# State-space scan and mixture of experts: another order of the first block, gates behind the first masked scores, T3 behind the masked scores

## The chip, the cores and the metric

The kernel runs on one core of one Trainium2 chip. Its time is device microseconds of one execution; the number compared is the median over runs. All data are float32.

## The reference, cut to what matters

The reference is two blocks in a row. The first is a chunked state-space scan (4 sequences, 8 heads, 768 steps, head width 32, state width 16):

```python
for c in range(nc):                       # chunks along the sequence
    cum = np.cumsum(log(clip(a)), axis=-1)
    L = np.exp(cum_i - cum_j) * causal
    y_intra = ((C @ B.T) * L) @ x
    y_inter = (C @ state) * np.exp(cum)
    y[chunk] = y_intra + y_inter
    state = np.exp(sum) * state + (B * decay_from_j).T @ x
```

The second takes y as 3072 tokens of width 256 and runs four experts over all of them, weighted by normalised probabilities:

```python
p = domain_probs / (domain_probs.sum(-1, keepdims=True) + 1e-09)
for e in range(4):
    h = np.maximum(x @ w1[e], 0.0)        # 256 -> 1024
    out += p[:, e:e + 1] * (h @ w2[e])    # 1024 -> 256
```

## The kernel before

The scan works in chunks of 128 steps: 24 chunks, four of which make a block of 512 tokens, six blocks in all. All eight heads of a chunk are done together. The experts work on a block in eight steps (four experts, two halves of the hidden width each), so there are 48 steps, numbered n. The order on every engine is written out by hand; no scheduler changes it, and each engine's queue runs in that order.

A chunk c passes these functions. `load_tokens` and `load_decays` put its DMAs on SyncE's queue (SP). Chunks 0 and 1 read their decays straight from the input and clip them on VectorE (DVE); the later ones read decays that the kernel has clipped itself, once for all chunks: the tile `a_sb` is loaded, clipped, copied to `a_cut` (whose first column is zeroed), and `store_decays` writes both to DRAM (`acut_d`, `ac_d`) through ScalarE's (ACT's) queue. `masks` (ACT) makes two masked copies of C, `scores` (TensorE, PE) the products of C and B, in four PSUM tiles. `decays` makes the matrix L by a scan on DVE (L241, tile LT, 1024 columns) and, for all but the first chunk of a sequence, a second scan (dec). `masked` (L285, DVE) multiplies the scores by L, which frees the PSUM tiles of the scores. `outputs` (L297, L303, PE) gives y, which ACT copies to `yT`; `carry` (DVE) brings the state on.

The gates are the normalised probabilities: four DVE instructions (L200 to L203) normalise the tile `pr`, `store_gates` transposes it on PE, copies it on ACT and writes it to DRAM (`p_d`), and `load_gate(k, e)` reads the rows of block k and expert e back, spread over all partitions.

An expert step of the steady loop multiplies in Strassen's form: seven products into the PSUM banks X and Y (`fmul`, L358), copies of X on ACT (`snap`), sums on DVE (`total`, L370), the rectified and gated hidden values on DVE (`gated`, L380), and differences of those (`diff`, L387: T3, T1, T2, T4), which feed the seven products of the second matrix (`smul`, L442) in the next step. `sums(k)` makes four sums and differences of `yT` for block k on DVE (L336 to L339). The weights' sums (`sum_w1`, `sum_w2`) are made once, in the first block, on GpSimd (POOL), and written back to DRAM.

The first two steps of the first block are done plainly, without Strassen's form: `plain_first` (L406) into banks X and Y, `plain_gated` (two instructions of L380, which free X and Y), `plain_second` (L423). They are interleaved with the scan of chunks 0 to 3, since y of the first half of the block is there after chunk 1.

In the steady loop, four of a block's eight steps also take in a chunk of the next block: `masks` and `decays` early in the step, `scores` and `masked` near its end. The last two of the four score tiles stand in the banks X and Y, so that the next step's first product, which writes X, waits until `masked` has read it:

```python
scores(c_in, ((ps_att, "att"), (ps_att, "att"), (ps_f, "X"), (ps_f, "Y")))
masked(c_in, (2, 3, 0, 1))
```

Of the kernel before, what the change touches and what calls it, by code (L numbers as in the profile page):

```python
# [8 lines left out]
FP32 = mybir.dt.float32  # L9
# [8 lines left out]
def kernel(  # L18
# [75 lines left out]
    def load_tokens(c):  # L94
        xb = load.tile([P, W], FP32, tag="xb", name="xb")
        nc.sync.dma_start(out=xb, in_=xbc[c])
        st.setdefault(c, {})["xb"] = xb

    def load_decays(c, queue):
        ab = load.tile([P, NH * P], FP32, tag="ab", name="ab")  # L100
        cut, whole = (a, a) if c < DIRECT else (acut_d, ac_d)
        nc.sync.dma_start(out=ab, in_=cut[c].rearrange("h s -> (h s)").partition_broadcast(P))
        st.setdefault(c, {})["ab"] = ab
        if c % chunks_per_seq:
            ah = st[c]["ah"] = load.tile([HN, P], FP32, tag="ah", name="ah")
            queue.dma_start(out=ah, in_=whole[c].unsqueeze(1).to_broadcast([NH, N, P]))
# [55 lines left out]

    pr = const.tile([P, T // P, E], FP32, name="pr")
    a_sb = const.tile([NCH * NH // 2, 2, P], FP32, name="a_sb")
    nc.scalar.dma_start(out=pr, in_=probs)
    nc.scalar.dma_start(
        out=a_sb, in_=a.rearrange("c h s -> (c h) s").rearrange("(p r) s -> p r s", r=2))
    load_decays(0, nc.sync)
    load_tokens(0)
    load_tokens(1)  # L170
    load_decays(1, nc.sync)


    ident = const.tile([P, NH, P], FP32, name="ident")
# [20 lines left out]
    def clip(v):  # L195
        nc.vector.tensor_scalar(out=v, in0=v, scalar1=1e-6, scalar2=1.0, op0=ALU.max, op1=ALU.min)


    total = const.tile([P, T // P, 1], FP32, name="total")
    nc.vector.reduce_sum(total, pr, axis=mybir.AxisListType.X)  # L200
    nc.vector.tensor_scalar_add(total, total, 1e-9)
    nc.vector.reciprocal(total, total)
    nc.vector.tensor_mul(pr, pr, total.to_broadcast([P, T // P, E]))  # L203

    nc.gpsimd.tensor_scalar(  # L205
        out=a_sb, in0=a_sb, scalar1=1e-6, scalar2=1.0, op0=ALU.max, op1=ALU.min)
    a_cut = const.tile([NCH * NH // 2, 2, P], FP32, name="a_cut")
    nc.gpsimd.tensor_copy(a_cut, a_sb)
    nc.gpsimd.memset(a_cut[:, :, 0:1], 0.0)

    def store_decays():
        nc.scalar.dma_start(
            out=acut_d.rearrange("c h s -> (c h) s").rearrange("(p r) s -> p r s", r=2), in_=a_cut)
        nc.scalar.dma_start(
            out=ac_d.rearrange("c h s -> (c h) s").rearrange("(p r) s -> p r s", r=2), in_=a_sb)

    def store_gates():
        rows = T // P * E
        pp = ps_att.tile([rows, P], FP32, tag="att", name="pp")
        nc.tensor.transpose(pp, pr.rearrange("p i e -> p (i e)"), ident[:, 0])  # L220
        p_sb = const.tile([rows, P], FP32, name="p_sb")
        nc.scalar.copy(out=p_sb, in_=pp)
        nc.scalar.dma_start(out=p_d.rearrange("i e s -> (i e) s"), in_=p_sb)
# [3 lines left out]
    def load_gate(k, e):  # L227
        g = gate[k, e] = ffn.tile([P, CPB, P], FP32, tag="gate", name="gate", bufs=3)
        nc.sync.dma_start(out=g, in_=p_d[CPB * k:CPB * k + CPB, e].partition_broadcast(P))
# [31 lines left out]
    def masks(c):  # L261

        s = st[c]
        m = s["ctm"] = att.tile([HN, NT, P], FP32, tag="ctm", name="ctm")
        for t in range(NT):
            nc.scalar.mul(m[:, t], s["xb"][:, OCT:OCT + P], tmask[:, t:t + 1])  # L266
# [14 lines left out]
    def masked(c, qs):  # L281
        s = st[c]
        for q in qs:
            h = slice(NT * q, NT * q + NT)
            nc.vector.tensor_mul(s["MT"][:, h, 0:P], s["g"][q], s["LT"][:, h])  # L285
# [3 lines left out]
    def outputs(c, pool, tag):  # L289

        s = st[c]
        first = c % chunks_per_seq == 0
        w = P + N if c % chunks_per_seq < chunks_per_seq - 1 else P
        xb, MT = s["xb"], s["MT"]
        y = pool.tile([P, NT, P + N], FP32, tag=tag, name="y")
        if not first:
            nc.tensor.matmul(  # L297
                out=y[:, :, 0:P], lhsT=state["M"].rearrange("p q d -> p (q d)"),
                rhs=s["cts"], start=True, stop=False, skip_group_check=True)
        for t in range(NT):  # L300
            for q in range(NQ):
                h = NQ * t + q
                nc.tensor.matmul(  # L303
                    out=y[32 * q:32 * q + 32, t, 0:w], lhsT=xb[:, h * D:h * D + D],
                    rhs=MT[:, NT * q + t, 0:w], start=(first and t == 0), stop=True,
                    tile_position=(0, 32 * q), skip_group_check=True)
        k, i = divmod(c, CPB)
        if i == 0:
            yT[k] = ffn.tile([P, NT, BLK], FP32, tag="yT", name="yT")
        nc.scalar.copy(out=yT[k][:, :, i * P:i * P + P], in_=y[:, :, 0:P])  # L310
        if w > P:
            s["A"] = att.tile([P, NT, N], FP32, tag="A", name="A")
            nc.scalar.copy(out=s["A"], in_=y[:, :, P:])
# [70 lines left out]
    def diff(n, o, x, y):  # L384
        h = hid[n]
        h[o] = ffn.tile([P, JJ, HB], FP32, tag="h" + o, name="h" + o)
        nc.vector.tensor_sub(h[o], h[x], h[y])  # L387
# [23 lines left out]
    def plain_gated(n, b):  # L411
        gated(n, f"1{b}", "X")
        gated(n, f"2{b}", "Y")
# [106 lines left out]
    warm = const.tile([P, 1], FP32, name="warm")  # L520
    nc.scalar.mul(warm, tmask[:, 0:1], tmask[:, 0:1])
    homes = ((ps_s, "acc0"), (ps_s, "acc1"), (ps_att, "att"), (ps_att, "att"))
    masks(0)
    scores(0, homes)
    store_gates()
    store_decays()
    load_decays(2, nc.sync)
    load_gate(0, 0)
    load_w2(0)
    load_w1(1)  # L530
    load_chunk(3)
# [2 lines left out]
    masked(0, range(NQ))  # L534
    masks(1)
    outputs(0, ps_att, "att")
    load_gate(0, 1)
    load_w1(2)
    load_w2(2)
# [13 lines left out]
    decays(2)  # L553
    carry(1)
    masked(2, range(NQ))
    plain_gated(0, 1)
    masks(3)
    outputs(2, ps_att, "att")
    load_chunk(5)

    scores(3, homes)
    plain_first(1, 1)
    decays(3)
    carry(2)
    masked(3, range(NQ))
    plain_gated(1, 1)
# [4 lines left out]
    plain_second(0, 1, 2)  # L571
    plain_second(1, 1, 1)
    plain_second(1, 1, 2)
    plain_first(0, 2)
    plain_gated(0, 2)
    sums(0)
    carry(3)
    sum_w1(3)
    sum_w1(0)
    sum_w2(3)  # L580
# [6 lines left out]
    for n in range(PLAIN, NS):  # L587
        k, r = divmod(n, SPB)

        enter, exit = ({2: 0, 3: 1, 5: 2, 6: 3}, {3: 0, 4: 1, 6: 2, 7: 3}) if k == 0 else (  # L590
            {0: 0, 2: 1, 4: 2, 6: 3}, {1: 0, 3: 1, 5: 2, 7: 3})
        c_in, c_out = (CPB * (k + 1) + d[r] if r in d and k < NBLK - 1 else None
                       for d in (enter, exit))
        ending = r == 0 and k > 0
        e = r // JJ
        if r % JJ == 0 and n + JJ < NS:
            load_gate(*divmod(n // JJ + 1, E))
        if n + 2 < NS:
            load_w1(n + 2)
            load_w2(n + 2)  # L600
        opened(n)
        total(n, 1, "11")
        gated(n, "11", "z11")
        if c_in is not None:
            masks(c_in)
            decays(c_in)
        for m in {2: (), 3: (4, 5)}.get(n, (n + 2,)):
            sum_w1(m)
            sum_w2(m)
        if r == 1 and k > 0:  # L610
            leave(k - 1, 0, BLK, both)
        smul(n - 1, 1)
        fmul(n, 6)
        snap(n, 6)
        smul(n - 1, 3)
        if ending:
            keep(k - 1, 0)
        if c_out is not None:
            outputs(c_out, ps_att, "att")
        fmul(n, 5)  # L620
        fmul(n, 7)
        snap(n, 7)
        total(n, 7, "22")
        smul(n - 1, 7)
        smul(n - 1, 5)
        if n == PLAIN:
            sum_w2(0)
            sum_w2(1)
        if ending:
            keep(k - 1, 1)  # L630
        gated(n, "22", "z22")
        if c_out is not None:
            carry(c_out)
            if c_out + 2 < NCH:
                load_chunk(c_out + 2)
        fmul(n, 3)
        total(n, 6, "12")
        fmul(n, 4)
        gated(n, "21", "X")
        gated(n, "12", "z12")  # L640
        if r == SPB - 1 and k < NBLK - 1:
            sums(k + 1)
        smul(n - 1, 6)
        diff(n, "T3", "22", "12")
        smul(n - 1, 2)
        if c_in is not None:
            scores(c_in, ((ps_att, "att"), (ps_att, "att"), (ps_f, "X"), (ps_f, "Y")))
            masked(c_in, (2, 3, 0, 1))
        if ending:
            combine(k - 1, 0)  # L650
            combine(k - 1, 1)
        smul(n - 1, 4)
        diff(n, "T1", "12", "11")
        diff(n, "T2", "22", "T1")
        diff(n, "T4", "21", "T2")
        if ending:
            combine(k - 1, 2)
# [46 lines left out]
```

## Time and profile before

| what | value |
|---|---|
| median of 4 runs | 668.65 us |
| lowest and highest run | 665.47 and 669.65 us |
| the profiled execution's own time | 665.47 us |
| its span, first to last instruction | 663.7 us |
| TensorE matmuls busy | 640.4 us, 96% |
| VectorE busy | 491.6 us, 74% |
| ScalarE, GpSimd busy | 114.1 and 108.5 us |
| DMA | 128.62 MB, mean 194 GB/s |

The profiled execution is one of the four runs. The busy times are unions of the instructions' intervals as the hardware profiler recorded them; weight loads (PEld) overlap matmuls and are counted apart. In the profile a line such as "PE X L358" means TensorE writing tile X at line 358 of the kernel, and "<-DVE h L380" that the wait was ended by DVE's instruction at line 380.

### The profile page before, as it was taken

Reading aid. Unit: us, or ns where it says so; the run is one execution under the profiler, and the core shown is the slowest. Engines: PE = TensorE matmul, PEld = TensorE weight load, DVE = VectorE, ACT = ScalarE, POOL = GpSimd, SP = SyncE. Lnnn points to the kernel's source line nnn. Section 1 sums busy time; section 2 is a strip of 40 time slices with the busy share of each in tenths; the row PEclk is TensorE's granted clock in tenths of the full one; section 3 lists DMA queues with packets and bytes.
Section 4 is the critical chain, followed back from the end, with each engine's and each line's share of the span. In section 5 each row is a group of like instructions: output and inputs, shape, how many; then the busy total and the mean of one; then the engine's idle time right before and its main releaser. Section 6 shows DMA issues by size and latency. Waiting matters only on the chain.

```text
span 663.7 us, 8687 instructions
## 1 busy us (share of the span) xinstructions
PE 640.4 (96%) x3321; PEld 537.0 (81%) x3321; DVE 491.6 (74%) x785; ACT 114.1 (17%) x244; POOL 108.5 (16%) x156
## 2 busy tenths in 40 slices
PE   3989999999999999999999999999999999999995
PEld 1777787888888888888888888888888888888884
DVE  7746989698687688866878867779868767856554
ACT  2101111122112121221122111112211211111110
POOL 4485685011000002000003000002100000200000
PEclk9989999999999999999999999999999999999999
DMA  6986999636736544765372865554573542562102
GB/s 227 346 329 229 312 324 332 238 140 176 279 135 216 186 181 113 280 226 178 123 260 89 258 199 194 194 183 163 169 280 119 193 170 114 149 247 112 55 1 32
DMA packets 70937, 128.62 MB, mean 194 GB/s; under 512 B 29040, under 2 KB 52464, under 8 KB 70896
## 3 DMA queue, kind: packets, MB, share of 16 engines
q1 hardware_dynamic: 65824, 112.74, 49.6%
q0 software_dynamic: 2304, 14.68, 5.6%
q10 hardware_dynamic: 2768, 0.66, 0.5%
q8 instruction: 26, 0.43, 0.3%
q14 instruction: 15, 0.12, 0.1%
HBM read 109.99 MB, written 18.07 MB: 193 GB/s over the span
## 4 chain that ended last, share of the span: by engine, by line
PE 91%; DVE 6%; DMA 1%; POOL 1%; issue 0%; ACT 0%; ACTq 0%; DVEq 0%; POOLq 0%
PE acc L442 40%; PE X L358 24%; PE Y L358 18%; PE y L303 2%; PE acc L423 2%; PE g L275 2%; DVE h L380 2%; PE y L297 1%; DVE hT L387 1%; PE X L406 1%; PE Y L406 1%; DMA a_sb<-in_a_dram 1%; DVE LT L241 1%; POOL a_sb L205 0%; DVE z L370 0%
## 5 line engine op out<-in xcount | busy, mean ns | idle before, releaser
L370 DVE TENSOR_TENSOR z<-Y,snap 128x512 f32<-128x512 f32 x138 | 95.0, 688 | 125.9 <-ACT snap L365 99.8
L442 PE MATMUL acc<-hT,wt 128*128 128x256 f32 x736 | 183.4, 382 | 0.8 <-DVE hT L387 0.8
L365 ACT COPY snap<-X 128x512 f32<-128x512 f32 x138 | 80.8, 585 | 472.0 <-PE X L358 470.0
L442 PEld LDWEIGHTS acc<-hT,wt 128*128 128x128 f32 x736 | 138.2, 190 | 25.5 <-issue 6.3
L358 PE MATMUL X<-yS,wt 128*128 128x256 f32 x552 | 141.7, 379 | 0.0
L442 PE MATMUL acc<-h,wt 128*128 128x256 f32 x552 | 141.5, 379 | 0.0
L358 PEld LDWEIGHTS X<-yS,wt 128*128 128x128 f32 x552 | 104.9, 190 | 14.3
L442 PEld LDWEIGHTS acc<-h,wt 128*128 128x128 f32 x552 | 104.9, 190 | 14.3
L380 DVE SCALAR_TENSOR_TENSOR h<-z,gate 128x512 f32<-128x512 f32 x138 | 98.3, 712 | 3.1
L358 PE MATMUL Y<-yT,wt 128*128 128x256 f32 x368 | 95.2, 381 | 0.3 <-DVE z L370 0.3
L358 PEld LDWEIGHTS Y<-yT,wt 128*128 128x128 f32 x368 | 69.4, 191 | 11.5 <-DVE z L370 0.7
L387 DVE TENSOR_TENSOR hT<-h,hT 128x512 f32<-128x512 f32 x92 | 70.7, 768 | 3.2
L387 DVE TENSOR_TENSOR hT<-h,h 128x512 f32<-128x512 f32 x92 | 63.4, 711 | 1.4
L248 POOL TENSOR_TENSOR MT<-xb,LT 128x128 f32<-128x128 f32 x20 | 8.7, 437 | 317.6 <-issue 167.9
L241 DVE TENSOR_TENSOR_SCAN LT<-ab,ident 128x1024 f32<-128x1024 f32 x24 | 54.8, 2284 | 1.4 <-DMA ab<-acut_d 1.0
L358 PE MATMUL X<-yT,wt 128*128 128x256 f32 x184 | 48.6, 387 | 4.2 <-DVE h L380 2.6
L358 PE MATMUL Y<-yS,wt 128*128 128x256 f32 x184 | 49.4, 391 | 0.2 <-DVE z L370 0.2
L380 DVE SCALAR_TENSOR_TENSOR h<-X,gate 128x512 f32<-128x512 f32 x50 | 34.5, 690 | 15.3 <-PE X L406 8.6
L358 PEld LDWEIGHTS X<-yT,wt 128*128 128x128 f32 x184 | 35.1, 193 | 10.5 <-DVE h L380 3.0
L358 PEld LDWEIGHTS Y<-yS,wt 128*128 128x128 f32 x184 | 33.2, 189 | 8.8 <-issue 3.9
L285 DVE TENSOR_TENSOR MT<-g,LT 128x256 f32<-128x256 f32 x96 | 33.9, 415 | 6.8 <-PE g L275 6.7
L275 PE MATMUL g<-ctm,xb 32*128 32x256 f32 x192 | 20.8, 461 | 7.7 <-ACT ctm L266 7.6
(75 smaller groups left out, 311.4 us busy)
## 6 DMA issues: line engine op xcount, KB each, us to landing
wt<-w_d SPq DMA_DIRECT2D x80, 896.0 KB, 6.4
w_d<-wt POOLq DMA_DIRECT2D x16, 896.0 KB, 5.9
ab<-acut_d SPq DMA_DIRECT2D x22, 512.0 KB, 6.3
wt<-in_w_dram SPq DMA_DIRECT2D x32, 256.0 KB, 6.3
xb<-in_xbc_dram SPq DMA_DIRECT2D x24, 320.0 KB, 5.0
gate<-p_d SPq DMA_DIRECT2D x24, 256.0 KB, 6.4
out_dram<-ot SPq DMA_DIRECT2D x40, 64.0 KB, 2.0
ah<-ac_d SPq DMA_DIRECT2D x19, 64.0 KB
```

The source lines that it names most:

```text
L241: nc.vector.tensor_tensor_scan(out=LT, data0=s["ab"], data1=ident.rearrange("p h s -> p (h s)"), initial=0.0, op0=ALU.mult, op1=ALU.add)
L275: nc.tensor.matmul(out=g.rearrange("p t s -> p (t s)"), lhsT=s["xb"][k, OBT:OBT + P], rhs=s["ctm"][k].rearrange("p t s -> p (t s)"), start ...
L285: nc.vector.tensor_mul(s["MT"][:, h, 0:P], s["g"][q], s["LT"][:, h])
L303: nc.tensor.matmul(out=y[32 * q:32 * q + 32, t, 0:w], lhsT=xb[:, h * D:h * D + D], rhs=MT[:, NT * q + t, 0:w], start=(first and t == 0), s ...
L358: nc.tensor.matmul(out=f[bank][:, j], lhsT=wt1[n][:, w, j * P:j * P + P], rhs=rhs, start=(i in (1, 2, 5) and j == 0), stop=(j == JJ - 1), ...
L365: nc.scalar.copy(out=s, in_=first[n]["X"])
L370: nc.vector.tensor_add(z, first[n]["Y"], first[n][i])
L380: nc.vector.scalar_tensor_tensor(out=h, in0=first[n][src], scalar=0.0, in1=g.unsqueeze(1).to_broadcast([P, JJ, HB]), op0=ALU.max, op1=ALU. ...
L387: nc.vector.tensor_sub(h[o], h[x], h[y])
L406: nc.tensor.matmul(out=f[bank][:, j], lhsT=wt1[n][:, w, j * P:j * P + P], rhs=yT[k][:, i, cols], start=(i == 0 and j == 0), stop=(i == 1), ...
L423: nc.tensor.matmul(out=acc[k, u][:, half], lhsT=w2_op(n, w)[:, j], rhs=hid[n][f"{i + 1}{b}"][:, j], start=(begins and i == 0 and j == 0), ...
L442: nc.tensor.matmul(out=acc[k, u][:, half], lhsT=w2_op(n, w)[:, j], rhs=rhs[:, j], start=(begins and j == 0), stop=(n % SPB == SPB - 1 and ...
```

## The change

It moves five things in the first block, and one in the loop.

- The load of the decays `a_sb` becomes the only one ahead on ACT's queue; the probabilities' load moves to SP's queue, behind the tokens and decays of chunks 0 and 1. The decays of chunk 1 are loaded ahead of its tokens.
- The clip, copy and memset of `a_sb` and `a_cut` move from GpSimd to DVE, ahead of chunk 0's clip, and `store_decays` moves ahead of the first `masks` on ACT.
- The four instructions that normalise the probabilities move into `store_gates`, and that and the first gate load move behind chunk 0's `masked`, chunk 1's `masks` and chunk 0's `outputs`.
- `decays(3)` moves ahead of `plain_gated(0, 1)`, which itself moves from behind `masked(2)` to behind `scores(3)`.
- `sums(0)` and `carry(3)` move ahead of `plain_first(0, 2)` and `plain_gated(0, 2)`.
- In every step of the loop that takes in a chunk, the difference T3 moves behind `scores` and `masked`.

Lines behind the first edits move by two: L285 before is L283 after, L358 is L356, L380 is L378.

```diff
-    nc.scalar.dma_start(out=pr, in_=probs)
     nc.scalar.dma_start(
         out=a_sb, in_=a.rearrange("c h s -> (c h) s").rearrange("(p r) s -> p r s", r=2))
     load_decays(0, nc.sync)
     load_tokens(0)
+    load_decays(1, nc.sync)
     load_tokens(1)
-    load_decays(1, nc.sync)
+    nc.sync.dma_start(out=pr, in_=probs)
...
-    total = const.tile([P, T // P, 1], FP32, name="total")
-    nc.vector.reduce_sum(total, pr, axis=mybir.AxisListType.X)
-    nc.vector.tensor_scalar_add(total, total, 1e-9)
-    nc.vector.reciprocal(total, total)
-    nc.vector.tensor_mul(pr, pr, total.to_broadcast([P, T // P, E]))
-
-    nc.gpsimd.tensor_scalar(
-        out=a_sb, in0=a_sb, scalar1=1e-6, scalar2=1.0, op0=ALU.max, op1=ALU.min)
+    clip(a_sb)
+
     a_cut = const.tile([NCH * NH // 2, 2, P], FP32, name="a_cut")
-    nc.gpsimd.tensor_copy(a_cut, a_sb)
-    nc.gpsimd.memset(a_cut[:, :, 0:1], 0.0)
+    nc.vector.tensor_copy(a_cut, a_sb)
+    nc.vector.memset(a_cut[:, :, 0:1], 0.0)
...
     def store_gates():
+        total = const.tile([P, T // P, 1], FP32, name="total")
+        nc.vector.reduce_sum(total, pr, axis=mybir.AxisListType.X)
+        nc.vector.tensor_scalar_add(total, total, 1e-9)
+        nc.vector.reciprocal(total, total)
+        nc.vector.tensor_mul(pr, pr, total.to_broadcast([P, T // P, E]))
         rows = T // P * E
...
+    store_decays()
     masks(0)
     scores(0, homes)
-    store_gates()
-    store_decays()
     load_decays(2, nc.sync)
-    load_gate(0, 0)
     load_w2(0)
...
     outputs(0, ps_att, "att")
+    store_gates()
+    load_gate(0, 0)
     load_gate(0, 1)
...
     masked(2, range(NQ))
-    plain_gated(0, 1)
     masks(3)
     outputs(2, ps_att, "att")
     load_chunk(5)
 
     scores(3, homes)
+    decays(3)
+    plain_gated(0, 1)
     plain_first(1, 1)
-    decays(3)
     carry(2)
...
+    sums(0)
+    carry(3)
     plain_first(0, 2)
     plain_gated(0, 2)
-    sums(0)
-    carry(3)
...
         smul(n - 1, 6)
-        diff(n, "T3", "22", "12")
         smul(n - 1, 2)
         if c_in is not None:
             scores(c_in, ((ps_att, "att"), (ps_att, "att"), (ps_f, "X"), (ps_f, "Y")))
             masked(c_in, (2, 3, 0, 1))
+        diff(n, "T3", "22", "12")
```

## The prediction

> **What bounds the kernel now.** I read the page first, then a table of windows, then TensorE's waits, then the timeline of the first 110 us.
>
> ```profile
> PE 640.4 (96%) x3321; PEld 537.0 (81%) x3321; DVE 491.6 (74%) x785; ACT 114.1 (17%) x244; POOL 108.5 (16%) x156
> PEclk9989999999999999999999999999999999999999
> ```
>
> TensorE (PE) is busy 640.4 of 663.7 us, so a change of order can win at most the 23.3 us in which it is not, and time lost to its clock. The dip to 8 in the third slice (33 to 50 us) is the only one. The windows show where the idle time lies:
>
> ```profile
> 0.00:10.00 10.00, 1.65 (x9) 0.67 (x9) 6.45 (x24) 2.27 (x4) 6.28 (x17) 1.00 0.80 273
> 10.00:20.00 10.00, 7.46 (x55) 4.29 (x55) 8.63 (x15) 2.35 (x9) 2.97 (x5) 1.00 0.71 214
> 40.00:50.00 10.00, 7.43 (x28) 5.93 (x27) 6.43 (x10) 1.18 (x3) 8.87 (x14) 0.83 0.70 278
> 60.00:70.00 10.00, 8.89 (x55) 6.52 (x55) 9.24 (x14) 2.22 (x6) 2.49 (x4) 1.00 0.80 290
> 46.27:49.67 3.40, 3.15 (x7) 2.50 (x8) 0.80 (x2) 1.03 (x3) 2.97 (x5) 0.50 0.52 198
> 300.00:400.00 100.00, 100.00 (x530) 84.20 (x530) 77.20 (x126) 18.70 (x40) 6.92 (x9) 1.00 0.56 191
> ```
>
> First comes the length of the stretch, then PE, weight loads, VectorE (DVE), ACT and POOL; the last three are granted clock, DMA share and GB/s. From 110 us on PE is full (100.00 of 100), so T3's new place can win nothing there. Idle are 8.35 us of the first ten, 2.54 of the next, 2.57 between 40 and 50 and 1.11 between 60 and 70; nearly all the rest is the tail after 600, untouched. TensorE's waits say on whom:
>
> ```profile
> PE X L358 <- DVE h L380: 2.6, 1, 2.6
> PE X L358 <- DVE MT L285: 1.6, 3, 1.0
> PE y L297 <- DVE MT L285: 1.3, 1, 1.3
> ```
>
> The timeline has the three places (start, duration, instruction, idle time before it and who ended it):
>
> ```profile
> 4.02 0.25 DVE L200 TENSOR_REDUCE total<-pr 128x24 f32<-128x96 f32 x1 [2.12 <-DMA pr<-in_probs_dram]
> 5.03 0.68 DVE L196 TENSOR_SCALAR ab<-ab 128x1024 f32<-128x1024 f32 x1
> 9.69 0.68 DVE L196 TENSOR_SCALAR ab<-ab 128x1024 f32<-128x1024 f32 x1
> 15.30 1.19 PE L297 MATMUL y<-cts,M 128*128 128x256 f32 x2 [1.33 <-DVE MT L285]
> 16.52 2.29 DVE L241 TENSOR_TENSOR_SCAN LT<-ab,ident 128x1024 f32<-128x1024 f32 x1 [1.03 <-DMA ab<-acut_d]
> 38.81 0.69 DVE L380 SCALAR_TENSOR_TENSOR h<-X,gate 128x512 f32<-128x512 f32 x1 [8.62 <-PE X L406]
> 41.14 0.71 DVE L336 TENSOR_TENSOR yS<-yT 128x256 f32<-128x256 f32 x1
> 45.79 0.68 DVE L380 SCALAR_TENSOR_TENSOR h<-X,gate 128x512 f32<-128x512 f32 x1
> 46.52 2.07 PE L358 MATMUL X<-yT,wt 128*128 128x256 f32 x4 [2.57 <-DVE h L380]
> 62.64 0.69 DVE L387 TENSOR_TENSOR hT<-h,h 128x512 f32<-128x512 f32 x1
> 63.72 1.13 PE L358 MATMUL X<-yT,wt 128*128 128x256 f32 x4 [0.96 <-DVE MT L285]
> 78.47 1.13 PE L358 MATMUL X<-yT,wt 128*128 128x256 f32 x4 [0.29 <-DVE MT L285]
> 106.32 1.13 PE L358 MATMUL X<-yT,wt 128*128 128x256 f32 x4 [0.34 <-DVE MT L285]
> ```
>
> In the chain of waits PE runs without a gap from 15.30 to 40.51. So whatever delays 15.30 delays everything to 40, and what speeds DVE in between wins nothing.
>
> **The start: the gates go onto the chain.** Before, DVE normalised the gates at 4.02, waiting for chunk 0's decays anyway. Now they stand between chunk 0's masked scores (8.36 to 9.78) and chunk 1's clip, 9.69 before. From the first gate instruction to the next clip is 5.03 - 4.02 = 1.01 us. Behind them in DVE's queue stand the clip, chunk 1's scan, decay, carry and masked scores, on which PE waits at 15.30. Chunk 1's scan stood at 10.67, 0.98 after its clip; chunk 0's scan followed its clip by 0.93, so 0.05 was POOL's delay, which goes. PE's start moves by 1.01 - 0.05 = +0.96, to 16.26. Bounds: 0 if the gates find a hole; more if probs land late. The probs' DMA now stands on SP behind chunk 1's tokens, and by the order view its issue waits for a DMA landing (a_sb's, as I read its slot), at about 4 us. At the page's medians of 5.0 to 6.4 us a transfer lands at 9 to 10.4, and DVE asks for it at 9.78: 0 to 0.6 us more. I take 0, because the probs themselves took from 0.74 to 4.0 before.
>
> The clip and copy of a_sb move from POOL (3.12 + 0.39 us) to DVE. The DVE clips took 0.68 us for 1024 columns and 0.20 for 128, so about 0.27 for 256; twice that and a memset of 0.07 make 0.6. They lie in DVE's 2.12 us of idle time if a_sb lands as the probs did, by 4.0, since its DMA takes the probs' place at the head of ACT's queue; then chunk 0's clip stays at 5.03. If it lands at 5.91 as before, DVE ends them at 6.5 and the clip is 1.5 late. I take 0 and keep 1.5 for the range.
>
> The decays' stores now issue at about 4.7 instead of 10.71. SP sat behind them from 5.46 to 12.54; the load of chunk 2's decays, which landed at 16.40, should now issue at 6.5 to 8 and land by 14 (the page's 6.3). Chunk 2's scan then follows chunk 1's masked scores directly, at 15.49 + 0.96 = 16.45 against 16.52. DVE has paid for the gates with its 1.03 us of waiting; PE has not. The transposed gates (0.42 on PE, 0.26 on ACT) stand behind chunk 0's outputs, where PE waits until 16 anyway. POOL is free 1.5 us earlier, which wins nothing. On SP the first gate load stands behind more weight loads, at about 15; with 6.4 us it lands at 21 to 22.
>
> **Scan 3 ahead of the first gated tile.** DVE ends chunk 2's masked scores at 21.8, then scan (2.29) and decay (0.40) to 24.5, then h from X (0.68) to 25.2. Bank X is wanted by the next plain_first at 25.16 + 0.96 = 26.1. Cost 0, with 0.9 us of cover; the gate at 21 to 22 is in time too. The scan needs chunk 3's decays, behind chunk 3's tokens on SP: issued at 12 to 13, plus 6.3, about 19.
>
> **Sums and carry moved up.** The largest term. Before, DVE idled 8.62 us, then did h, h, the four sums and the carry (41.14 to 45.8), and only then the h from X that frees the bank for PE at 46.52. PE had ended its last plain_first at 43.95: 2.57 us idle. Now the 4.7 us of sums and carry run when chunk 3's yT is copied, at 32.0 + 0.96 = 33.0, until 37.7, still inside the idle time (plain_first(0,2) ends X at 38.8 + 0.96 = 39.8). The gated tiles follow PE one by one, and PE goes on at once: -2.57.
>
> The clock adds to it: the window of 46.27 to 49.67 was granted 0.50, hence the 0.83 of the window. In the chain the eight matmuls after 46.52 take 2.07 + 1.46 = 3.53 us, where the same eight take 0.86 + 0.86 = 1.72 later: 1.81 us, which goes with the gap. I take -1.81; the bound is 0, if a typical run does not fall into that state.
>
> [...] (That the start is cold shows in durations alone: the pair y L297 takes 1.19 us at 15.30 and 0.59 at 22.73.)
>
> **T3 down.** In four steps of the first block DVE does T3 between the gated tiles and the masked scores that free bank X. Moving T3 behind them takes it from PE's wait: 0.61 (its step to the next instruction, 62.64 to 63.25) of the 0.96, and the whole 0.29 and 0.34: -1.24. T3 itself ends 1.4 us later, which is covered: its matmuls stand at 71.13, T3 would end near 64.8. If that cover were gone PE would pay 1.4 a step. Bounds: 0 if DVE is the limit behind it (9.62 of 10 busy at 100 to 110), 1.6 at most.
>
> **Sum:** +0.96 - 2.57 - 1.81 - 1.24 = -4.66 us: the profiled execution's span 663.7 to 659.0 and its time, 1.8 above its span, 665.47 to 660.8. That execution is the fastest of four; their median is 668.65, and the same shift gives 664.0. Nothing in the profile explains the 3.2 us between them.
>
> **Rivals.** [...] (2) The start costs nothing, or T3 frees more: -5.6 or better, 663 or less. For: DVE's chain has hidden slack of 1.03. Against: PE's own wait at 15.30 names masked scores behind the gates. (3) Slower: SP's new waits hold chunk 3's decays. The scan now stands ahead of h, which frees X for PE; each microsecond of landing after 22.8 (21.8 + 0.9 cover) is one on PE, and beyond 22.8 + 4.66 = 27.4 the kernel is slower: at 31, 672.2. Against: they landed at 23.65 before although SP was blocked until 12.54. (4) That the change does not do what it says is excluded: the order view shows every move.
>
> **How the numbers follow.** Forecast (-3.4 to -5.6) 0.57; rival 1 0.27; rival 2 0.08; rival 3, with late probs, 0.08. A change under 0.5% (3.3 us) is about what a measurement of this kernel cannot tell from none. Faster by more: 0.57 + 0.08, less 0.02 for the edge, 0.63. Slower by more: 0.05. Within: 0.32. The range reaches from 661.0 (a gain of 7.6: rival 2 and the runs' spread) to 668.3 (rival 1 with a late a_sb); above and below it lies 0.2.
>
> **What would show it.** Right: PE's wait on h L380 of 2.6 us gone, no clock under 1 near 45, the PE start near 16.3, chunk 2's scan without DMA wait, waits of X on MT under 0.4 in all. Wrong: PE's first y L297 after 17.5 or before 15.4, a DVE wait on pr, a wait of LT on ab above 1 us near 22, or a gap of PE between 20 and 45.

## The result, and the profile after

The changed kernel's median is 666.73 us against 668.59 for the kernel before. The ratio of the two kernels' runs is 0.9976, with a 95% interval [0.9969, 0.9984]: 1.6 us faster. That is inside the 0.5% that was called no change. The direction was right; of the forecast 4.66 us about a third came. The profiled execution of after took 666.93 us (span 665.2), close to its median. The profiled execution of before was the fastest of its four, so absolute positions in the two traces can't be subtracted as if both were usual.

The page's lines and the windows of after, with the columns as before:

```profile
PE 641.0 (96%) x3321; PEld 537.4 (81%) x3321; DVE 494.4 (74%) x788; ACT 114.1 (17%) x244; POOL 111.0 (17%) x153
PEclk9999999999999999999999999999999999999999
```

```profile
40.00:50.00 10.00, 10.00 (x47) 8.57 (x46) 3.92 (x7) 1.17 (x3) 6.71 (x11) 1.00 0.46 184
60.00:70.00 10.00, 9.34 (x57) 7.10 (x57) 9.66 (x15) 2.42 (x7) 4.12 (x6) 1.00 0.74 262
46.27:49.67 3.40, 3.40 (x16) 2.75 (x15) 1.27 (x2) 1.17 (x3) 2.92 (x6) 1.00 0.51 205
300.00:400.00 100.00, 99.83 (x529) 84.01 (x528) 76.05 (x126) 18.16 (x39) 6.91 (x9) 1.00 0.55 186
```

The hole between 40 and 50 us is gone (7.43 busy before, 10.00 now), the dip of the clock with it (0.50 granted from 46.27 to 49.67 before, 1.00 now). What is new is small and far away: between 300 and 400 us PE was busy 100.00 and now is 99.83. The waits of after say on whom; the first line is DVE's, the others PE's (total in us, count, longest in us):

```profile
DVE MT L283 <- PE g L273: 20.2, 18, 1.1
PE Y L356 <- DVE z L368: 3.3, 8, 0.6
PE X L356 <- DVE MT L283: 0.7, 2, 0.5
```

and the same of before:

```profile
DVE MT L285 <- PE g L275: 6.7, 17, 0.4
PE Y L358 <- DVE z L370: 0.5, 2, 0.3
```

The wait on h of 2.6 us is gone, as forecast, and X waits for MT 0.7 us instead of 1.6; under 0.4 was forecast. But PE's wait for z, from which bank Y comes free, went from 0.5 to 3.3 us, and DVE's own wait for the scores from 6.7 to 20.2. The timeline of after around the start (start, duration, instruction, idle time and what ended it):

```profile
5.04 0.29 DVE L196 TENSOR_SCALAR a_sb<-a_sb 96x256 f32<-96x256 f32 x1 [3.15 <-DMA a_sb<-in_a_dram]
5.70 0.69 DVE L196 TENSOR_SCALAR ab<-ab 128x1024 f32<-128x1024 f32 x1
10.36 0.24 DVE L212 TENSOR_REDUCE total<-pr 128x24 f32<-128x96 f32 x1
11.37 0.69 DVE L196 TENSOR_SCALAR ab<-ab 128x1024 f32<-128x1024 f32 x1
16.92 1.19 PE L295 MATMUL y<-cts,M 128*128 128x256 f32 x2 [3.30 <-DVE MT L283]
17.20 2.29 DVE L239 TENSOR_TENSOR_SCAN LT<-ab,ident 128x1024 f32<-128x1024 f32 x1
```

The gates take 11.37 - 10.36 = 1.01 us of DVE's chain, just as computed, and the probabilities were there in time. Chunk 2's scan has no DMA wait any more. But a_sb landed at 5.04 and not by 4.0, so chunk 0's clip begins 0.67 later than 5.03, and y starts at 16.92, 1.62 after the 15.30 of before.

### The profile page after: what moved, and what is told of

Its sections match the earlier page's. It is cut to its first block, busy times and chain, and to the rows that moved or that the text cites. A ratio compares the mean times of both kernels' runs of the same rounds, so it can differ in the third digit from the quotient of the medians.

```text
span 665.2 us, 8685 instructions
## 1 busy us (share of the span) xinstructions
PE 641.0 (96%) x3321; PEld 537.4 (81%) x3321; DVE 494.4 (74%) x788; ACT 114.1 (17%) x244; POOL 111.0 (17%) x153
## 4 chain that ended last, share of the span: by engine, by line
PE 87%; DVE 8%; issue 1%; ACT 0%; DVEq 0%
PE acc L440 38%; PE X L356 22%; PE Y L356 17%; DVE hT L385 3%; PE g L273 2%; PE acc L421 2%; PE y L301 2%; DVE MT L283 1%; PE X L404 1%; PE y L295 1%; DVE z L368 1%; PE Y L404 1%; DVE h L378 1%; DVE LT L239 1%; DVE o L468 0%
## 5 line engine op out<-in xcount | busy, mean ns | idle before, releaser
L356 PE MATMUL X<-yS,wt 128*128 128x256 f32 x552 | 141.7, 379 | 0.0
L356 PEld LDWEIGHTS X<-yS,wt 128*128 128x128 f32 x552 | 104.9, 190 | 14.3
L378 DVE SCALAR_TENSOR_TENSOR h<-z,gate 128x512 f32<-128x512 f32 x138 | 98.7, 715 | 3.1
L356 PE MATMUL Y<-yT,wt 128*128 128x256 f32 x368 | 94.8, 380 | 0.4 <-DVE z L368 0.3
L356 PEld LDWEIGHTS Y<-yT,wt 128*128 128x128 f32 x368 | 68.6, 190 | 11.9 <-DVE z L368 1.2
L356 PE MATMUL Y<-yS,wt 128*128 128x256 f32 x184 | 49.4, 391 | 3.0 <-DVE z L368 3.0
L283 DVE TENSOR_TENSOR MT<-g,LT 128x256 f32<-128x256 f32 x96 | 34.0, 416 | 20.4 <-PE g L273 20.2
L356 PE MATMUL X<-yT,wt 128*128 128x256 f32 x184 | 47.4, 380 | 0.7 <-DVE MT L283 0.7
L356 PEld LDWEIGHTS Y<-yS,wt 128*128 128x128 f32 x184 | 33.2, 189 | 11.9 <-DVE z L368 5.2
L378 DVE SCALAR_TENSOR_TENSOR h<-X,gate 128x512 f32<-128x512 f32 x50 | 34.5, 691 | 9.5 <-PE X L356 5.7
L356 PEld LDWEIGHTS X<-yT,wt 128*128 128x128 f32 x184 | 34.8, 190 | 6.1 <-DVE MT L283 1.5
```

Of the source, the lines that this page charges most:

```text
L356: nc.tensor.matmul(out=f[bank][:, j], lhsT=wt1[n][:, w, j * P:j * P + P], rhs=rhs, start=(i in (1, 2, 5) and j == 0), stop=(j == JJ - 1), ...
L378: nc.vector.scalar_tensor_tensor(out=h, in0=first[n][src], scalar=0.0, in1=g.unsqueeze(1).to_broadcast([P, JJ, HB]), op0=ALU.max, op1=ALU. ...
```

## The experiments

Results of all twelve, each against runs of the kernel before on the same chip (its median was 668.58 to 668.75 there). After itself stands at 0.9976 [0.9969, 0.9984].

| kernel | median us | ratio to before |
|---|---|---|
| e1: after, T3 back in its old place | 665.69 | 0.9944 [0.9923, 0.9966] |
| e2: before, T3 down alone | 669.86 | 1.0011 [0.9995, 1.0027] |
| e3: before, sums and carry up alone | 666.67 | 0.9964 [0.9949, 0.9979] |
| e4: before, the start's edits alone | 668.55 | 0.9997 [0.9977, 1.0016] |
| e5: after, T3 down in block 0 alone | 664.39 | 0.9947 [0.9931, 0.9964] |
| e6: e5 with 68 idle matmuls at the start | 667.62 | 0.9983 [0.9974, 0.9993] |
| e7: e1 without normalising | 664.31 | 0.9941 [0.9928, 0.9954] |
| e8: before without normalising | 668.13 | 1.0003 [0.9986, 1.0021] |
| e9: e1 with 31 idle matmuls | 664.03 | 0.9933 [0.9912, 0.9955] |
| e10: e1, scan 3 back too | 666.13 | 0.9964 [0.9946, 0.9982] |
| e11: e5 with 31 idle matmuls | 662.18 | 0.9909 [0.9888, 0.9931] |
| e12: e11, T3 down in block 0's first loop step alone | 662.92 | 0.9914 [0.9894, 0.9934] |

**e1 and e2: T3 undone, and T3 alone.** The edit of e1 on after; e2 makes the opposite one on before.

```diff
         smul(n - 1, 6)
+        diff(n, "T3", "22", "12")
         smul(n - 1, 2)
...
             masked(c_in, (2, 3, 0, 1))
-        diff(n, "T3", "22", "12")
```

> The changed kernel with T3 back in its old place. Theory A (T3's new place costs time: DVE now idles until the scores are there, and total's z, which frees bank Y, comes late in the steady loop): TensorE's waits on z fall from 3.3 us to under 0.8, DVE's idle time before MT from 20 to about 7 us, waits of X on MT rise from 0.7 to about 1.5; about 2.4 us faster than the changed kernel, 664.3, ratio to the kernel before 0.9935. Rival A' (the waits on z come from TensorE being earlier after the sums were moved): z waits stay near 3 us, X on MT rises by 0.8, 667.5, ratio 0.9985.

> The kernel before with T3 alone moved behind the masked scores. Theory A: waits on z of about 3 us appear in the steady loop, those of X on MT fall from 1.6 to 0.7: about 2 us slower than before, 670.6, ratio 1.003. Rival A': 0.9 us to 1.2 us faster, 667.5, ratio 0.998, z waits as before (0.5).

Taking T3 back makes after faster: 0.9944 against 0.9976, intervals just apart, 2.1 us. T3 alone makes before slower by 0.7 us, an interval that reaches to no change. So T3's move, forecast to win 1.24 us, loses 2.1 us in the changed kernel; on top of before the loss is smaller and not clear of noise. The waits of e1 and then of e2 show the exchange:

```profile
DVE MT L283 <- PE g L273: 6.7, 17, 0.4
PE X L356 <- DVE MT L283: 2.1, 3, 1.5
PE Y L356 <- DVE z L368: 0.5, 2, 0.3
```

```profile
DVE MT L285 <- PE g L275: 21.1, 20, 1.1
PE Y L358 <- DVE z L370: 3.6, 8, 0.8
PE X L358 <- DVE MT L285: 0.5, 1, 0.5
```

Wherever T3 stands behind the masked scores, X's wait shrinks by 1.1 to 1.4 us and Y's wait on z is about 3 us longer. How it comes about is seen in DVE's timeline near 144 us, in the first step of the second block, before:

```profile
144.55 0.69 DVE L387 TENSOR_TENSOR hT<-h,h 128x512 f32<-128x512 f32 x1
145.63 1.42 DVE L285 TENSOR_TENSOR MT<-g,LT 128x256 f32<-128x256 f32 x4 [0.40 <-PE g L275]
...
151.21 0.68 DVE L370 TENSOR_TENSOR z<-Y,snap 128x512 f32<-128x512 f32 x1
```

and after:

```profile
145.42 1.42 DVE L283 TENSOR_TENSOR MT<-g,LT 128x256 f32<-128x256 f32 x4 [1.12 <-PE g L273]
146.76 0.68 DVE L385 TENSOR_TENSOR hT<-h,h 128x512 f32<-128x512 f32 x1
147.36 0.42 DVE L460 TENSOR_TENSOR u<-acc,kept 128x256 f32<-128x256 f32 x1
...
151.60 0.68 DVE L368 TENSOR_TENSOR z<-Y,snap 128x512 f32<-128x512 f32 x1
```

The masked scores wait for the scores on PE, not for DVE. T3 (0.69 us) filled that wait; now the wait stands empty (0.40 becomes 1.12) and T3 comes behind it. All that follows on DVE, the next step's z among it, is that much later relative to PE, z frees Y, and PE waits:

```profile
152.34 1.13 PE L356 MATMUL Y<-yS,wt 128*128 128x256 f32 x4 [0.55 <-DVE z L368]
257.61 1.13 PE L356 MATMUL Y<-yS,wt 128*128 128x256 f32 x4 [0.60 <-DVE z L368]
362.94 1.13 PE L356 MATMUL Y<-yS,wt 128*128 128x256 f32 x4 [0.17 <-DVE z L368]
467.79 1.13 PE L356 MATMUL Y<-yS,wt 128*128 128x256 f32 x4 [0.18 <-DVE z L368]
```

Before, the first of these four groups had no wait, at 151.95. These four lines are all that T3's move costs PE in the later blocks, 1.5 us in sum; the other four of the eight waits on z, 1.8 us in sum, lie in the first block. Of the 16 steps of the later blocks that take in a chunk, PE waits in four, one in each block: its first step, in which DVE also adds up the output of the block before (u in the timeline above) and has no idle moment between T3 and z. In the other twelve T3 comes late too, but PE does not wait; there DVE has idle time further on, and between 110 and 600 us its wait for ACT's copies (snap) fell from 79.9 to 70.4 us.

**e3, e4 and e10: sums, start, scan.** e3 moves only `sums(0)` and `carry(3)`; e4 makes only the first three points of the change on before; e10 takes scan 3 back out of e1.

```diff
+    sums(0)
+    carry(3)
     plain_first(0, 2)
     plain_gated(0, 2)
-    sums(0)
-    carry(3)
```

```diff
-    nc.scalar.dma_start(out=pr, in_=probs)
...
+    nc.sync.dma_start(out=pr, in_=probs)
...
+    clip(a_sb)
...
+    store_decays()
     masks(0)
     scores(0, homes)
-    store_gates()
-    store_decays()
...
     outputs(0, ps_att, "att")
+    store_gates()
```

```diff
     masked(2, range(NQ))
+    plain_gated(0, 1)
...
     scores(3, homes)
-    decays(3)
-    plain_gated(0, 1)
     plain_first(1, 1)
+    decays(3)
```

> The kernel before with only sums(0) and carry(3) moved up. Theory: the gap of 2.57 us before the first Strassen step is gone, and with it the half-speed stretch near 46 us: 2.6 us faster if only the gap counts in a typical run, 4.4 if the clock does too: 664.2 to 666.0, ratio 0.9934 to 0.9961; TensorE's first y L297 stays at 15.3. Rival (the stall only moves: DVE is late for the gated tiles or the loop waits later): less than 1.5 us faster, above 667.1.

> The kernel before with only the start changed (loads, decays' clip and stores, gates). Theory B (the gates cost 0.96 us and the late landing of a_sb 0.67 us, on TensorE's path): first y L297 at 16.9, about 1.6 us slower, 670.2, ratio 1.0024. Rival (DVE's wait for chunk 2's decays, 1.03 us, was on the path, so the start costs 0 to 0.6): 668.6 to 669.2, ratio under 1.001.

> The changed kernel with T3 back and with scan 3 and the first gated tile in their old order, so the start and the sums alone are left of the change. My prediction's cover: scan 3's new place costs and wins nothing, ratio 0.9944 as with it. Rival (scan 3's place wins, because masked scores of chunk 3 come earlier; start and sums alone measured 0.9997 and 0.9964): 0.996.

The sums win 2.4 us [1.4, 3.4], not 4.38. The start's edits cost nothing: -0.2 us, with an interval from -1.5 to +1.1 that just holds the forecast +0.96 too. Together (e10) they give what the sums give alone. Putting scan 3 up as well (e1 against e10) wins 1.3 us by the ratios, whose intervals overlap, so that they don't show it, and 0.7 by the two traces: e1's X at 79.27 us is 0.82 ahead of e10's at 80.09, of which 0.15 is an earlier first y (17.12 against 17.27).

Two traces say more. This is the timeline of e3, which has the start of before:

```profile
5.70 0.25 DVE L200 TENSOR_REDUCE total<-pr 128x24 f32<-128x96 f32 x1 [3.80 <-DMA pr<-in_probs_dram]
6.71 0.69 DVE L196 TENSOR_SCALAR ab<-ab 128x1024 f32<-128x1024 f32 x1
16.93 1.19 PE L297 MATMUL y<-cts,M 128*128 128x256 f32 x2 [1.26 <-DVE MT L285]
```

The probabilities landed at 5.70 here, against 4.02 in the profile of before, DVE reached the first clip 1.7 us later, and y began at 16.93, where after has it too (16.92). In e2, the other trace with all of before's start, the probabilities landed at 5.86 and y began at 17.09; in the five traces with after's start and no idle matmuls (after, e1, e4, e5, e10) it began between 16.92 and 17.66. The start that the forecast took for usual was an early one.

PE's waits of e4 and then of e3 show why the sums won less:

```profile
PE X L356 <- DVE h L378: 1.7, 1, 1.7
PE X L356 <- DVE MT L283: 1.7, 2, 1.4
```

```profile
PE X L358 <- DVE MT L285: 2.7, 3, 1.8
```

The stall on h was 1.7 in e4 (1.8 in e2), not 2.57. It is as long as DVE makes it: the four sums and the carry took 4.65 us in the trace of before (41.14 to 45.79), 3.79 in e4 and 3.87 in e2, because some of the same instructions took longer there, for a reason that no run shows. And once it is gone (e3), X waits for MT 2.7 us, where before had 1.6 and e4 1.7: PE arrives earlier at chunk 4's masked scores, about 64 us, and DVE is not ready. The clock's part was smaller too. The eight matmuls of the first Strassen step, up to the start of the next ones, took 49.89 - 46.52 = 3.37 us in before and 48.82 - 46.90 = 1.92 in after: 1.45 us for the half-speed stretch, not 1.81.

```profile
49.89 1.89 PE L423 MATMUL acc<-h,wt 128*128 128x256 f32 x8
```

```profile
46.90 1.03 PE L356 MATMUL X<-yT,wt 128*128 128x256 f32 x4
48.82 1.89 PE L421 MATMUL acc<-h,wt 128*128 128x256 f32 x8
```

A stall of 1.75 and up to 1.45 for the clock, less the 1.1 that comes back at chunk 4's masked scores, make up to 2.1. The measured 2.4 [1.4, 3.4] allows that; no run separates the three.

**e5: T3 down in the first block alone.**

```diff
+        if k > 0:
+            diff(n, "T3", "22", "12")
         smul(n - 1, 2)
...
+        if k == 0:
+            diff(n, "T3", "22", "12")
```

> The changed kernel with T3 behind the masked scores in the first block alone, in its old place from the second block on. Theory A (in the steady loop T3 fills the time in which DVE waits for the scores; in the first block DVE is behind TensorE and bank X is the wait): waits on z under 1.5 us, of X on MT under 1 us; faster than the version with T3 back everywhere (ratio 0.9944) by 0.5 to 1.2 us, ratio 0.993. Rival (T3's gain in the first block is lost to the wait on z that follows there): no faster than 0.9944.

0.9947 against e1's 0.9944. PE's waits of e5:

```profile
PE Y L356 <- DVE z L368: 1.8, 4, 0.5
PE X L356 <- DVE MT L283: 0.7, 2, 0.5
```

X's 2.1 become 0.7 and Y's 0.5 become 1.8: in the first block alone the new place gives what it takes. What after loses, 1.9 us by the ratios (0.9947 to 0.9976), is lost in the later blocks, where X had no wait that T3's move could cut; the four waits there make 1.5 of it.

**e7 and e8: no normalising.** Both leave out the four instructions that normalise the probabilities (`reduce_sum`, add, `reciprocal`, `tensor_mul`), e7 in e1, e8 in before.

```diff
-    nc.vector.reduce_sum(total, pr, axis=mybir.AxisListType.X)
-    nc.vector.tensor_scalar_add(total, total, 1e-9)
-    nc.vector.reciprocal(total, total)
-    nc.vector.tensor_mul(pr, pr, total.to_broadcast([P, T // P, E]))
```

> The changed kernel with T3 back, without the four instructions that normalise the probabilities (that part of the computation is left out). Theory B1 (in the new place they are on the path by 0.95 us): first y L295 0.95 us earlier, 16.0, about 0.9 us faster than with them (ratio 0.9944), 0.993. Rival (DVE waits anyway): 0.9944.

> The kernel before without the four normalising instructions (that part of the computation is left out). Theory B2 (in a usual run the probabilities land at about 5.7 us, after chunk 0's decays, so the instructions hold chunk 0's clip by about 1.2 us in their old place too; the profiled run, where they ran at 4.02, is an early one): first y L297 near 15.8 instead of 17, 1 us faster than before, ratio 0.9985. Rival (they lie in idle time, as I predicted): ratio 1.000, y L297 unchanged.

Without them y starts at 15.93 in e7 (17.12 in e1) and at 16.17 in e8 (16.93 in e3, which shares before's start). So these instructions stand on the path of the first y in both places, for about 1.0 us (1.2, of which 0.2 is an earlier first clip in e7) and 0.8 us: the move replaced one cost by another of nearly the same size. Whether an earlier first y is worth time stays open: e8 gained nothing (1.0003), with a stall on h of 2.3 us, while e7's trace is still 1.2 us ahead of e1's at 63 us, with a ratio (0.9941) too wide to tell it.

**e6 and e9: idle matmuls at the start.** The traces of after and e1 had shown the first expert matmuls slow: eight of them took 3.33 and 3.78 us, where eight take 1.99 later. Matmuls on zeros, written into the still unused bank X, fill PE's idle time before and between the first scores: 28, 12 and 28 of them in e6 (on e5), 12, 6 and 13 in e9 (on e1).

```diff
+    heat(12)        # nc.tensor.matmul on zeros, 128 columns each
     scores(0, homes)
+    heat(6)
...
     scores(1, homes)
+    heat(13)
```

> The same with 68 idle matmuls (128x128 by 128 columns of constants, into bank X, result unused) on TensorE ahead of its first scores, behind them, and behind chunk 1's scores, where TensorE waits anyhow. Theory C (TensorE's clock, granted in full only at 23.7 to 26.3 us, makes the stretch from 17 us on last longer, half of 6.5 to 9 us): full clock before 17 us, y, scores and plain_first at full speed from 17 on, 3 to 4.5 us faster than without, ratio 0.987, if DVE keeps up. Rival C' (DVE's scans and masked scores are the bound there, so a faster TensorE waits for them): less than 1.5 us faster, new waits of y on MT.

> The changed kernel with T3 back in its old place, and idle matmuls cut to fit TensorE's waits: 12 ahead of the first scores, 6 behind them, 13 behind chunk 1's scores (each takes two records of 0.11 us at the full clock, 0.21 at half). Theory C (the half-speed start costs time): full clock from about 6 us, first y L295 at 16.9 to 17.2 as without them, first Strassen step at 44 instead of 46.9 to 48.3, 2 to 4 us faster than without (ratio 0.9944): 0.989 to 0.991. Rival C' (DVE binds in that stretch): gaps of over 1 us on TensorE between 20 and 44, ratio above 0.993.

e6 was too large: each call is two records, the idle matmuls pushed the first scores from 7.6 to 9.9 us and y to 21.8, and the kernel lost against e5. In e9 the first scores, at 7.52 us, took 0.71 us, where after's, at 7.40, took 1.24, and the first Strassen step came at 44.50 instead of e1's 48.25, 3.75 us earlier; the time gained only 0.0011, within the error. The timeline and the window of e9 show where the lead went:

```profile
61.76 1.13 PE L356 MATMUL X<-yT,wt 128*128 128x256 f32 x4 [2.46 <-DVE MT L283]
```

```profile
62.80:66.20 3.40, 3.40 (x10) 2.69 (x9) 3.30 (x6) 1.18 (x3) 0.57 (x1) 0.50 0.71 249
```

PE came to chunk 4's scores early and waited 2.46 us for DVE instead of 1.48 (e1), and behind that wait the clock was halved for 3.4 us.

**e11 and e12: both together.** If that wait eats the lead, T3 down at that step, where DVE is late, should free it: e11 is e5 with e9's idle matmuls, e12 the same with the move in one step alone:

```diff
-        if k > 0:
+        if n > PLAIN:
             diff(n, "T3", "22", "12")
...
-        if k == 0:
+        if n == PLAIN:
             diff(n, "T3", "22", "12")
```

> The 31 idle matmuls as fitted, with T3 behind the masked scores in the whole first block, in its old place after it. The first fitted version won 3.9 us by 45 us and lost 2.5 of it at the first Strassen step's end, where bank X waits 2.46 us for the masked scores. If DVE's queue is what is late there, T3's new place takes 0.65 us off that wait and costs up to 1.5 in waits on z later in the block: ratio 0.993 to 0.996 (0.9933 without). If the half-speed window after that wait goes too: 0.991.

> The same with T3 behind the masked scores in the first Strassen step alone, the one where bank X waits longest. If the loss on z comes from the later steps only, this keeps the 0.65 us and costs nothing: ratio 0.992; first wait of X on MT near 1.8 instead of 2.46, waits on z under 0.6. Rival (what T3 leaves is taken by z of the next step at once): 0.9933 or above.

PE's waits of e11:

```profile
PE X L356 <- DVE MT L283: 0.8, 1, 0.8
PE Y L356 <- DVE z L368: 1.1, 3, 0.6
```

e11 took 662.18 us, 0.9909 [0.9888, 0.9931], e12 the same within the error: about 6 us faster than before and 4.5 faster than after. X's wait of 2.46 us is 0.77 in e11, and the half-speed stretch behind that wait is gone there: the clock column shows 1.00 from 60 to 70 us, and the two groups of four matmuls behind the wait's own take 1.03 us each, where e9's took 1.84 and 1.91. e12's profiled execution has a mean clock of 0.999. The same place of T3 that loses about 2 us over the whole kernel seems worth about 1.6 (0.9933 to 0.9909, intervals overlapping) where DVE is the limit.

## Why the prediction was right and wrong

**Sum of parts.** With ratios times 668.6 us:

| part | forecast us | measured us |
|---|---|---|
| start: gates, a_sb, stores (e4) | +0.96 | -0.2 |
| sums and carry up: gap and clock (e3) | -2.57 - 1.81 | -2.4 |
| scan 3 up (e1 against e10) | 0 | -1.3, intervals overlapping; by traces -0.7 |
| T3 down (after against e1) | -1.24 | +2.1 |
| whole | -4.66 | -1.6; the parts sum to -1.8 |

**T3 is the step that failed, by sign.** It was forecast as -1.24 with bounds of 0 to 1.6 gained. The part that was argued, X's wait on MT, came: 0.9 us less in the two profiles, 1.4 against e1. What was overlooked is in the sentence "From 110 us on PE is full ..., so T3's new place can win nothing there": it can lose there. The cover named was T3's own matmuls at 71.13; the row that mattered was DVE's wait "MT L285 <- PE g L275: 6.7, 17, 0.4", which says that DVE waits for PE at this very point, 17 times. An instruction moved behind such a wait leaves it empty, and everything on DVE behind it is late, not the moved one alone; PE pays where DVE has no idle time left before its next z. In the first block the new place was worth nothing (e5 against e1: 0.9947 and 0.9944), because 1.3 us of waits on z came for 1.4 us of waits on MT; in the later blocks it cost 1.9 us. The price named, "1.4 a step" if the cover is gone, was not paid: PE's waits on z were 0.17 to 0.60 us.

**Sums and carry: mechanism right, size wrong.** The gap and the dip near 46 went, and the sums run in DVE's idle time, as written. The term was taken from the fastest execution, with a stall of 2.57; those of e2 and e4 had 1.8 and 1.7, e8 2.3. The clock's 1.81 added up durations that overlap: by the starts of the matmuls it was 1.45. And "what is late next" was not asked of this term: 1.1 us of it reappears at chunk 4's masked scores.

Nor was the clock's part the sums' alone. In the traces a run's mean granted clock is 0.997 to 0.999 without a half-speed stretch ahead of the kernel's end, and 0.995 with one (before, e4, e9). It was 0.995 or less in 63 of the 80 runs of before beside the experiments and in none of after, so the whole change did win the clock back. But it was so in 3 of 12 runs with the sums up alone (e3), in 7 of 12 with start and sums (e10), and in 3 of 12 with T3 down alone (e2), whose stall on h is still there. In the traces the stretch follows the stall on h once (before) and X's wait for the masked scores twice (e4, e9); e2 and e8, with a stall on h of 1.8 and 2.3 us, have a mean clock of 0.997 in their profiled executions, as traces without such a stretch do.

So rival 1, to which the forecast gave 0.27 and by which the clock gives nothing because typical runs have no half-speed stretch near 46 us, was right about that place in three of the four traces that have the stall (e2, e4, e8), and wrong that the clock gives nothing; that the gain stayed so far under the forecast is T3's doing. The upper end of the range, 668.3, does not follow from the terms named for it, the clock's 1.81 and the 1.5 for a late a_sb: 664.0 + 1.81 + 1.5 is 667.3.

**Start: right in its parts, wrong in what it was set against.** The gates took 1.01 us of DVE's chain as computed. The bound kept for a late a_sb (+1.5) was partly used: +0.67. But in e3, whose start is before's, the probabilities hold DVE until 5.70 and y starts where after's does: there the gates stood on the same path in their old place. Whether they delayed the clip in the profile of before too, where they ran "waiting for chunk 0's decays anyway", its trace does not show. The sentence "Nothing in the profile explains the 3.2 us between them" was the warning: the profile was not of a usual execution, and an early start by 1.6 us, with full speed at about 19 us instead of near 24 as in after, fits that difference. That is argued from other kernels' traces and not shown; before was profiled once only.

**Scan 3** cost nothing, as said, and may have won a little that was not foreseen. **Rival 3**, chunk 3's decays late, did not happen: LT has no wait on ab there. Of the wrong signs listed none came, because none of them was a sign for T3; for T3 only a right sign was listed (X on MT under 0.4; it went to 0.7), while the loss stood in another wait.

**When the clock falls** the runs do not settle. Gaps of 2.57 us (before) and 2.46 us (e9) each went with 3.4 us at 0.50, from 46.27 and from 62.80. In e4 a stall on h of 1.72 us was passed at full clock, and a shorter one behind it, 1.36 us at MT, was not:

```profile
49.38 1.13 PE L356 MATMUL X<-yT,wt 128*128 128x256 f32 x4 [1.72 <-DVE h L378]
65.44 2.08 PE L356 MATMUL X<-yT,wt 128*128 128x256 f32 x4 [1.36 <-DVE MT L283]
```

```profile
48.04:51.44 3.40, 2.06 (x10) 1.83 (x11) 1.85 (x4) 0.89 (x3) 3.00 (x5) 1.00 0.44 173
61.69:65.09 3.40, 2.24 (x13) 1.05 (x11) 3.11 (x5) 0.00 (x0) 3.06 (x4) 1.00 0.65 266
65.10:68.50 3.40, 3.06 (x7) 2.52 (x8) 3.26 (x7) 0.94 (x3) 1.79 (x3) 0.50 0.41 103
```

The windows are as long as the half-speed stretch. In the first, which holds most of the stall on h, PE was busy 2.06 us, and matmuls at full speed followed (1.03 us for four at 50.35); in the second, just ahead of the half-speed stretch, it was busy 2.24 us. So here neither the length of the stall nor the busy time in such a window alone decides it. The second window holds the small matmuls of the scores; whether that matters no run tried.

## What to carry to other kernels

Before an instruction is moved behind another one, look at what that other one waits for: if it waits for another engine, the moved instruction was free filler in that wait, and all behind it gets late in every iteration of the loop, not only in the stage that was to gain. Then look for the iterations in which the engine has no idle time left: here four of 16 paid. A local gain is taken locally: with PE ahead (e11, e12) the same move seemed worth something in the first block, and in the later blocks it lost time. And when the profiled execution is clearly faster than the median, bound its terms by what a usual start would do to them, and ask of each gap that is closed which wait stands next.

## What the runs showed of the hardware that was not expected

TensorE ran at about half speed for microseconds after its unbroken work began (in after the two matmuls of y took 1.19 us at 16.92 and 0.59 at 25.85), and how long varied. The eight matmuls of a plain first step (L404, L406 in before) take 1.99 us at full speed. In after the first ones took longer:

```profile
20.96 3.33 PE L404 MATMUL X<-yT,wt 128*128 128x256 f32 x8
24.12 1.89 PE L404 MATMUL Y<-yT,wt 128*128 128x256 f32 x8
28.27 1.99 PE L404 MATMUL X<-yT,wt 128*128 128x256 f32 x8
```

In e1 they took 3.78 us and the next eight 2.63. So full speed came near 24 us in after and near 26 in e1, 7 and 9 us after PE's unbroken work began (16.92 and 17.12), in before, where the first eight took 1.99 us at 19.18, at about 19, some 4 us after 15.30, and in e5, where the first eight took 1.99 us at 21.08, within 4 us of 17.17. The windows' clock column shows 1.00 for those first stretches (after from 12 to 20 and 20.30 to 23.60 us), though the durations are up to nearly doubled (3.33 and 3.78 us against 1.99), so here the durations tell the speed. With thirty-one idle matmuls in PE's waiting time the first scores, at 7.52 us, already ran at full speed (0.71 us, 1.24 in after; e9), and with DVE's wait shortened at the same time they were worth about 2.5 us (e5 to e11, 0.9947 to 0.9909, intervals that touch), against 1.6 for the whole change under study. The first DMA landings vary as well: the same load of the probabilities was there at 4.02 us in one execution (before) and at 5.70 in another (e3).
